# Mixer kernel on one core: all channel groups of five batches by block products, and a written order for the engines

## The chip, the core and the metric

The kernel runs on one core of a Trainium2 chip. A core has five engines that run at once, each through its own list of instructions in order: TensorE (PE, matrix products into PSUM; its weight loads are shown apart as PEld), VectorE (DVE), ScalarE (ACT), GpSimd (POOL) and SyncE (SP, which here only starts transfers). PSUM has eight banks of 512 fp32 columns. Engines wait for one another by semaphores. The metric is the device time of one execution in microseconds: the median of several runs.

## The reference

Inputs are q, k and v of shape 8 x 8 x 576 x 64 (batch, head, token, head column) and four weight matrices, all fp32. For each batch and head a linear attention is computed:

```python
phi(x) = where(x > 0, x, exp(x) - 1) + 1
kv  = phi(k)^T v                 # 64 x 64 per head
z   = sum of phi(k) over tokens
x   = (phi(q) kv) / (phi(q) z + 1e-6)
```

The heads of a batch side by side make x, 576 tokens by 512 channels. Then follows a mixer:

```python
h  = max(x^T w_tok1, 0) w_tok2   # 576 -> 256 -> 576, over tokens
u  = x + h^T
h2 = max(u w_ch1, 0) w_ch2       # 512 -> 1536 -> 512, over channels
out = u + h2
```

`max(u w_ch1, 0)` is called the first channel mixing here and the product with `w_ch2` the second.

## The kernel before, in words

Everything is computed in bf16 with fp32 sums. A batch's 576 tokens are four blocks of 128 (the main part) and 64 more; the 64 of two batches are handled together as one block of 128 (the "tails": `mm2_tails`, `mm3_tail`, `mm3_tails`, `tail_product`, `mm4` with t = 8).

The steps for batch n are these. SP loads q, k and v in halves of 576 KB (`load`), each into one fp32 buffer for all batches from 2 on. `phi_exp` (L148) takes the exponential on ScalarE, `phi_add` (L154) and `phi_end` (L161) finish phi on VectorE as min(exp(x), max(x + 1, 1)); `e` has four buffers, `y` two. `vcast` (L174) casts v. `kv` (L184) multiplies on TensorE, ScalarE copies the sums. From batch 2 on phi(q) is transposed by a DMA from SP's queue (`qtr_dma`, L219). `nd_all` (L252) makes numerators and denominators on TensorE and divides on VectorE. `mm1` (L306) and `mm2` (L317) mix over tokens; VectorE adds x to give u, and a transposing DMA (`utr_dma`, L519) makes uT.

The first channel mixing has twelve column blocks of 128, each four matmuls of 512 columns (`mm3`, L535), read by a ScalarE activation that clamps at zero (L550) into `cr`. Its output can also be computed by blocks: the inner 512 channels, the 1536 output channels and the tokens are each cut in two, and instead of eight block products seven are formed of sums and differences of blocks (a Winograd form of Strassen's method). The 1536 columns make three groups of 2 x 256 for this. In batches 2 to 6 the kernel does so for group 2 only (`mix_one`, L702): sums of weight blocks are made once (`group_sums`, L696, into `swc`), four sums of u blocks per batch (`u_sums`, L686, into `tuc`), then per group seven products of four matmuls of 256 columns. Products 1, 6 and 5 are copied to fp32 `part` buffers by ScalarE (L720), 4 is clamped by ScalarE (L718), and 2, 3 and 7 are read by VectorE, which adds the copied part and clamps (`add_relu`, L530). In batch 7 all three groups are done in this way (`mix_first`, L730).

The second channel mixing of batches 1 to 7 uses seven products too (`pair_product`, L839; `product`, L755): `row_sums` (L657) makes sums of `cr` blocks on VectorE into `sb`, which lies in the buffers of batch 1's v and q. For batches 1 to 6 ScalarE copies three partial products (`pair_copy`, L856), VectorE adds u (`pair_end`, L859), POOL adds the copies (L863), and POOL's queue writes the batch out in two transfers of 512 KB (`pair_put`). The output buffer `obuf` has eight slots, given out in turn. Batch 0 has a direct second mixing (`mm4`), and its first mixing too is direct.

The order of the work is the order in which the code issues it. Up to batch 6 `run` (L1060) walks a list of large TensorE pieces and issues, behind piece i, the smaller steps put at i (numbers such as `put(7, ...)`). The last batch follows a string of short names, `SEQUENCE` (L873). PSUM banks come from two rings, or from small tables. Batch 7's outputs leave in 24 transfers of 64 KB from SP's and ScalarE's queues (`product_read`, L798; `tail_read`, L834).

Of the kernel before, what the change touches and what calls it, by code (L numbers as in the profile page):

```python
# [15 lines left out]
EPS = 1e-6  # L16


@with_exitstack
def kernel(  # L20
# [43 lines left out]
    ring = {1: 0, 2: 0}  # L64

    def bank(at=None):
        if at is None:
            at, ring[1] = ring[1], (ring[1] + 1) % 4
        return psum[:, at]

    def banks(at=None):
        if at is None:
            at, ring[2] = 4 + ring[2], (ring[2] + 2) % 4
        return psum[:, at:at + 2]

    def two16():
        return banks().bitcast(BF16).rearrange("p a (t s) -> p a t s", s=128)
# [24 lines left out]
    uTj = [t.rearrange("p r j c -> p (r j c)").rearrange("p (j r c) -> p j r c", j=NDM, r=R) for t in uT]  # L102
    uTt = const("uTt", [128, 2, NDM, 128])
    cr = [const(f"cr{b}", [128, NCH, SM]) for b in range(2)]
    crt = const("crt", [128, NCH, 128])
    obuf = const("obuf", [128, 8, DM], FP32)
    swc = const("swc", [128, 4, 2, 256])
# [31 lines left out]

    live = {}  # L140
    o_at = [0]

    def o_slots(m):
        at = o_at[0] if o_at[0] + m <= 8 else 0
        o_at[0] = (at + m) % 8
        return obuf[:, at:at + m]

    def phi_exp(nm, n, j0, nj):  # L148
        f = raw[nm, rb(n)][:, j0:j0 + nj].rearrange("p j f -> p (j f)")
        e = work.tile([128, 2 * TD], BF16, name="e", tag="e", bufs=4)[:, :nj * TD]  # L150
        nc.scalar.activation(out=e, in_=f, func=AF.Exp)  # L151
        live["e", nm, n, j0] = e

    def phi_add(nm, n, j0, nj):  # L154
        f = raw[nm, rb(n)][:, j0:j0 + nj].rearrange("p j f -> p (j f)")
        y = work.tile([128, 2 * TD], BF16, name="y", tag="y")[:, :nj * TD]
        nc.vector.tensor_scalar(out=y, in0=f, scalar1=1.0, scalar2=1.0, op0=ALU.add, op1=ALU.max)  # L157
        for j in range(nj):
            live["y", j0 + j] = y[:, j * TD:]

    def phi_end(nm, n, j0, nj):  # L161
        c, i = divmod(j0, 2)
        dst = (kp if nm == "k" else qp)[:, c, :, i:i + nj]
        e, y = live["e", nm, n, j0], live["y", j0][:, :nj * TD]
# [4 lines left out]
    def phi(nm, n, c):  # L169
        phi_exp(nm, n, 2 * c, 2)  # L170
        phi_add(nm, n, 2 * c, 2)
        phi_end(nm, n, 2 * c, 2)
# [39 lines left out]
    def qtr(n, c, put=nc.scalar.copy):  # L212
        tp = two16()
        for h, ts in enumerate(TS):
            qtr_mm(c, ts, tp[:, h])
# [1095 lines left out]
```

## Time and profile before

| | us |
|---|---|
| median of 3 runs (lowest to highest) | 247.29 (247.22 to 247.83) |
| span of the profiled execution, first to last instruction | 246.4 |
| TensorE busy | 236.1 |
| VectorE busy | 198.8 |
| ScalarE busy | 139.3 |
| GpSimd busy | 76.9 |
| first mixing of batch 2 begins | 86.3 |
| first mixing of batch 7 begins | 214.3 |
| last VectorE addition begins | 242.7 |

No other time of the profiled execution is given than its span. The profile's page gives busy times, the span in 40 slices (tenths busy), the transfer queues, the chain of work that ended last, and the costliest groups of instructions by line. The views asked besides are a table of busy time by stage, the timeline of one engine, the waits, and the chain in order of time. Busy time of TensorE is not work at full rate, since matmuls overlap: the distance from one start to the next is its pace. The same holds for VectorE, where an instruction starts up to 0.1 us before the one in front has ended.

### The profile page before, as it was taken

What the parts mean: (1) busy time and instruction counts of PE and PEld (TensorE: products, weight loads), DVE (VectorE), ACT (ScalarE), POOL (GpSimd) and SP (SyncE); (2) the same over time, 40 slices, a digit from 0 to 9 for tenths busy, and PEclk for the clock granted to TensorE, in tenths of its full rate; (3) what the DMA queues carried; (4) which work ended last, traced back from release to release, by engine and by line L of the source; (5) the groups of instructions that cost most, each with busy time, mean ns of one, the idle gap of its engine ahead of it and who ended that gap; (6) DMA issues with size and microseconds to landing.
All of it is one profiled execution on the core that took longest, in us unless ns stands there. A gap on an engine that the chain in (4) does not pass through costs nothing.

```text
span 246.4 us, 6090 instructions
## 1 busy us (share of the span) xinstructions
PE 236.1 (96%) x2477; PEld 162.3 (66%) x2496; DVE 198.8 (81%) x349; ACT 139.3 (57%) x224; POOL 76.9 (31%) x88
## 2 busy tenths in 40 slices
PE   7789999999999899999999999999999999999993
PEld 3475455564868456865678556865676567888883
DVE  5955877889799998988894499979996779956973
ACT  4673881569774367736897167656852652175100
POOL 9670030296703600061004500071007700440360
PEclk9999999999999999999999999999999999999999
DMA  6999999999726796589979955459748702352055
GB/s 248 267 203 258 348 275 308 355 251 289 294 24 133 223 334 271 132 224 210 358 263 174 412 148 192 93 115 329 228 89 94 170 3 43 64 112 61 4 127 130
DMA packets 50444, 48.40 MB, mean 196 GB/s; under 512 B 30192, under 2 KB 36720, under 8 KB 50416
## 3 DMA queue, kind: packets, MB, share of 16 engines
q1 hardware_dynamic: 41984, 35.00, 48.2%
q0 software_dynamic: 7472, 12.22, 22.7%
q10 hardware_dynamic: 960, 0.79, 1.4%
q8 instruction: 19, 0.31, 0.5%
q14 instruction: 9, 0.07, 0.1%
HBM read 35.85 MB, written 9.44 MB: 184 GB/s over the span
## 4 chain that ended last, share of the span: by engine, by line
PE 84%; DVE 6%; DMA 5%; issue 3%; ACT 1%; SPq 0%; DVEq 0%
PE ps L543 22%; PE ps L852 18%; PE ps L712 6%; PE ps L312 6%; PE ps L583 5%; PE ps L740 4%; PE ps L768 4%; PE ps L325 4%; DMA q_raw<-in_q_dram 3%; PE ps L557 2%; PE ps L570 2%; DMA uT<-u 2%; PE ps L820 2%; PE ps L261 2%; PE ps L191 1%
## 5 line engine op out<-in xcount | busy, mean ns | idle before, releaser
L543 PE MATMUL ps<-uT,wc 128*128 128x512 bf16 x252 | 60.2, 379 | 0.8 <-DMA uT<-u 0.5
L550 ACT ACTIVATE cr<-ps 128x512 bf16<-128x512 f32 x59 | 34.7, 600 | 32.9 <-PE ps L543 32.7
L543 PEld LDWEIGHTS <-wc 128*128 128x128 bf16 x256 | 24.1, 98 | 25.1 <-DMA uT<-u 0.8
L863 POOL TENSOR_TENSOR obuf<-obuf,q_raw 128x512 f32<-128x512 f32 x6 | 8.1, 1344 | 93.3 <-DVE obuf L861 59.1
L852 PE MATMUL ps<-k_raw,v_raw 128*128 128x256 bf16 x216 | 24.9, 273 | 0.0
L852 PEld LDWEIGHTS <-v_raw 128*128 128x128 bf16 x216 | 21.0, 98 | 3.9 <-issue 0.4
L852 PEld LDWEIGHTS <-cr 128*128 128x128 bf16 x216 | 21.1, 98 | 3.7
L861 DVE TENSOR_TENSOR obuf<-ps,u 128x512 f32<-128x512 f32 x24 | 16.3, 685 | 8.1 <-PE ps L852 5.8
L151 ACT ACTIVATE e<-q_raw 128x1152 bf16<-128x1152 f32 x16 | 18.3, 1163 | 7.3 <-DVE x L244 5.5
L151 ACT ACTIVATE e<-k_raw 128x1152 bf16<-128x1152 f32 x16 | 18.2, 1165 | 2.7 <-DMA k_raw<-in_k_dram 2.7
L852 PE MATMUL ps<-wc,cr 128*128 128x256 bf16 x144 | 17.7, 273 | 0.0
L276 DVE TENSOR_TENSOR x<-ps,dens 128x768 bf16<-128x768 f32 x18 | 17.2, 953 | 0.4
L655 DVE TENSOR_TENSOR v_raw<-cr 128x768 bf16<-128x768 bf16 (+2 forms) x24 | 14.8, 617 | 2.1 <-ACT cr L718 2.1
L337 DVE TENSOR_TENSOR u<-ps,x 128x1024 bf16<-128x1024 f32 x12 | 14.6, 1217 | 0.4 <-PE ps L325 0.3
L176 ACT CAST vs<-v_raw 128x1152 bf16<-128x1152 f32 x12 | 13.5, 1161 | 0.0
L312 PE MATMUL ps<-x,w 128*128 128x512 bf16 x49 | 13.0, 379 | 0.3
L165 DVE TENSOR_TENSOR qp<-e,y 128x1152 bf16<-128x1152 bf16 x16 | 11.9, 753 | 1.6 <-ACT e L151 0.9
L165 DVE TENSOR_TENSOR kp<-e,y 128x1152 bf16<-128x1152 bf16 x16 | 12.7, 816 | 0.5 <-ACT e L151 0.4
L157 DVE TENSOR_SCALAR y<-k_raw 128x1152 bf16<-128x1152 f32 x16 | 11.7, 763 | 1.3 <-DMA k_raw<-in_k_dram 1.3
L157 DVE TENSOR_SCALAR y<-q_raw 128x1152 bf16<-128x1152 f32 x16 | 12.4, 793 | 0.4 <-DMA q_raw<-in_q_dram 0.4
L325 PE MATMUL ps<-ar,w2p 128*128 128x512 bf16 x44 | 11.8, 379 | 0.3
L583 PE MATMUL ps<-wc,cr 128*128 128x512 bf16 x47 | 11.9, 379 | 0.1
(182 smaller groups left out, 458.8 us busy)
## 6 DMA issues: line engine op xcount, KB each, us to landing
k_raw<-in_k_dram SPq DMA_DIRECT2D x16, 576.0 KB, 7.6
q_raw<-in_q_dram SPq DMA_DIRECT2D x16, 576.0 KB, 5.9
v_raw<-in_v_dram SPq DMA_DIRECT2D x14, 576.0 KB, 9.2
out_dram<-obuf POOLq DMA_DIRECT2D x12, 512.0 KB, 6.9
wc<-in_moe_w_ch_dram POOLq DMA_DIRECT2D x8, 384.0 KB, 9.8
out_dram<-obuf POOLq DMA_DIRECT2D x4, 256.0 KB, 6.0
out_dram<-obuf ACTq DMA_DIRECT2D x12, 64.0 KB, 2.2
out_dram<-obuf SPq DMA_DIRECT2D x12, 64.0 KB, 1.9
```

Of the source, the lines that this page charges most:

```text
L151: nc.scalar.activation(out=e, in_=f, func=AF.Exp)
L157: nc.vector.tensor_scalar(out=y, in0=f, scalar1=1.0, scalar2=1.0, op0=ALU.add, op1=ALU.max)
L165: live["phi"] = nc.vector.tensor_tensor(out=dst.transpose([0, 2, 1, 3]), in0=e.rearrange("p (i t d) -> p i t d", i=nj, t=T), in1=y.rearran ...
L276: nc.vector.tensor_tensor(out=xv[:, :, rc0:rc0 + 3], in0=v_[m][:, :, k0:k0 + 6, 0:D].rearrange("p i (q a) d -> p i q a d", a=2), in1=den.r ...
L312: nc.tensor.matmul(out=ps[:, mt], lhsT=w1t[:, b, ms] if r == R else w1[:, r, ms], rhs=x[b][:, r, :], start=(r == 0), stop=(r == R))
L325: nc.tensor.matmul(out=ps[:, i], lhsT=w2v(kt, r, b), rhs=ar[b][:, kt, :], start=(kt == 0), stop=(kt == NT - 1 and not add))
L543: nc.tensor.matmul(out=ps, lhsT=wc1[:, kj, 128 * mc:128 * mc + 128], rhs=uTj[b][:, kj] if n < 2 else uT[b][:, :, kj], start=(kj == 0), sto ...
L550: nc.scalar.activation(out=cr[b][:, mc, :], in_=ps, func=AF.Relu)
L583: nc.tensor.matmul(out=ps, lhsT=crt[:, kc, :] if t == 8 else cr[b][:, kc, 128 * r:128 * r + 128], rhs=wc2[:, kc, :], start=(kc == 0), stop ...
L655: return engine.tensor_tensor(out=s_[which - 1][:, ks], in0=x_, in1=y_, op=op)
L852: nc.tensor.matmul(out=live[tile_][:, j], lhsT=lhs[:, k_], rhs=rhs[:, k_], start=(first and j == 0 and k_ == 0), stop=(k_ == KH - 1), skip ...
L861: nc.vector.tensor_tensor(out=o, in0=live[tile_], in1=u[n % 2][:, d::2, HC[c]], op=ALU.add)
```

## The change

1. In batches 2 to 6 all three groups of the first channel mixing go by seven block products (`mix_mm`, `mix_read`), where before only group 2 did. `swc` holds weight sums of three groups (`GSW`). Groups 0 and 1 keep their copied parts in the first 2 KB per partition of each of the four row-sum buffers (`HOLD`), group 2 in `part` as before.
2. The issuing of every step is cut into small named tokens (`put`), and one string, `ORDER`, lists all of them after the setup; it replaces the lists and `SEQUENCE`. A token name is the batch, a letter for the step and an index: `4x26` is product 6 of group 2 of batch 4, `4y26` its read, `5gu1` the addition that makes half of batch 5's u, `5uT1` its transposing DMA, `4s2` a sum of u blocks, `4w10` a row sum, `4eW` an output addition, `6Lk0` a load. The order differs from before on every engine and on the queues of SP and POOL. Batch 1's loads are issued in the order k, v, q (before: k, q, v).
3. The PSUM bank of every result is named in a table (`BANK`), likewise output slots (`SLOT`), exp buffers (`EBUF`) and y buffers (`YBUF`). `obuf` has six slots (before eight), `e` three buffers (four), `y` one (two). The pair outputs of batches 1 to 6 all use slots 0 to 3.
4. The row sums 1 and 2 of batches 2 to 6 are cut into blocks of 2 and 4 (before 3 and 3).
5. Batch 7's outputs leave in 16 transfers: where `WHOLE` names a row of blocks, both halves of the columns go in one transfer of 128 KB, after the later half is done.

```diff
+NO = 6
+NE = 3
+NY = 1
+GSW = {2: 0, 1: 1, 0: 2}
+HOLD = {2: 'p0 p1 p2', 1: 's2 s3 s2', 0: 's0 s1 s0'}
+CUTS = {1: [0, 3, 6], 2: [0, 2, 6], 3: [0, 2, 6], 4: [0, 2, 6], 5: [0, 2, 6], 6: [0, 2, 6], 7: [0, 2, 4, 6]}
+GATE = {'1k0': ('wc1', 0), '2q0': ('wc2', 1), '4q0': ('u', 2, 1), '7q0': ('u', 5, 1)}
+ON_DVE = {'1v0', '2v1', '0r3', '0r6', '0r9', '1r5', '1r8'}
+WHOLE = {'00', '01', 't0', 't1'}
...
+1Lk0 1Lk1 1Lv0 A40 1Lv1 A41 1Lq0 A42 A43 1Lq1 0ma0 At2 0ma1 At3 0ma7
...
+5o0 5ne 6Lv1 4y11 4x25 3eW 4x21 6qx0 5n2 3hW 3p41 4y21 3p40 5n1 W1 4x01 4y25 5o1 4x26 6kb0 4y01 4x02 4y26 3eX
+4x16 6qx1 4x12 4y02 3o 4x27 6qa1 4x06 4y16 4x15 4y12 4y06 4x17 6qb1 4y15 4x05 6v0 6qa0 4x07 4x23 4y27 5f0 4y05
...
+    def mix_mm(n, g, i):
+        first = i in (1, 2, 5)
         b = n % 2
+        ps = mix_tile(n, g, i)
+        if n == B - 1:
+            s_, t, c0 = sw, tu, 256 * g
+        else:
+            s_, t, c0 = [swc[:, GSW[g], w] for w in range(4)], tuc, 0
+        w_ = lambda m, h: cblock(m, h)[:, :, 256 * g:]
         lhs, rhs = {1: (w_(0, 0), ublock(0, 0, b)), 2: (w_(0, 1), ublock(1, 0, b)),
+                    3: (s_[3][:, :, c0:], ublock(1, 1, b)), 4: (w_(1, 1), t[3]),
+                    5: (s_[0][:, :, c0:], t[0]), 6: (s_[1][:, :, c0:], t[1]),
+                    7: (s_[2][:, :, c0:], t[2])}[i]
...
+    def mix_read(n, g, i):
+        ps = mix_tile(n, g, i)
+        if n == B - 1:
+            c1, c6, c5 = hold[g]
         else:
+            c1, c6, c5 = [hold_at[w[0]][int(w[1])] for w in HOLD[g].split()]
+        dst = lambda m, e: cr[n % 2][:, KH * m + 2 * g:KH * m + 2 * g + 2, HALF[e]]
         if i == 4:
             nc.scalar.activation(out=dst(1, 0), in_=ps, func=AF.Relu)
         elif i in (1, 6, 5):
...
+    def product_put(n, i, j, e):
+        o = slots(f"{n}P{j}", 2)
+        d, c = {2: (0, 0), 7: (1, 1), 3: (0, 1), 4: (1, 0)}[i]
+        w = slice(0, 512) if f"{j}{d}" in WHOLE else HC[c]
+        [nc.sync, nc.scalar][e].dma_start(out=outv[n, :, 2 * (2 * j + d) + e, w],
+                                          in_=o[half[e], d, w])
...
+    for name in ORDER.split():
+        tok[name]()
```

## The prediction

> **What bounds the kernel now.** I read the page's busy table and its forty slices first.
>
> ```profile
> span 246.4 us, 6090 instructions
> ...
> PE 236.1 (96%) x2477; PEld 162.3 (66%) x2496; DVE 198.8 (81%) x349; ACT 139.3 (57%) x224; POOL 76.9 (31%) x88
> ...
> PE   7789999999999899999999999999999999999993
> ...
> DVE  5955877889799998988894499979996779956973
> ACT  4673881569774367736897167656852652175100
> ...
> PEclk9999999999999999999999999999999999999999
> ...
> PE 84%; DVE 6%; DMA 5%; issue 3%; ACT 1%; SPq 0%; DVEq 0%
> ```
>
> TensorE is the bound: 96% busy, 84% of the chain, full clock. But VectorE's row is almost as dense in the middle, so I asked for the busy time by stage, cut where a batch's first channel mixing begins (columns: stage, length, then busy time and count of PE, PEld, DVE, ACT, POOL).
>
> ```profile
> 53.30:86.30 33.00, 32.12 (x434) 21.07 (x436) 30.45 (x48) 22.38 (x34) 17.03 (x18) 1.00 0.69 206
> 86.30:109.17 22.87, 22.77 (x229) 15.90 (x232) 21.16 (x35) 15.35 (x23) 3.32 (x4) 1.00 0.75 233
> 109.17:139.15 29.98, 29.82 (x333) 20.87 (x334) 22.27 (x37) 20.14 (x30) 7.21 (x8) 1.00 0.95 275
> 139.15:164.41 25.26, 25.16 (x277) 17.15 (x278) 22.75 (x38) 16.47 (x25) 3.98 (x5) 1.00 0.59 171
> 164.41:189.60 25.19, 24.60 (x272) 16.83 (x272) 21.97 (x37) 14.47 (x23) 5.56 (x6) 1.00 0.75 182
> 189.60:214.33 24.73, 24.62 (x206) 16.66 (x209) 20.83 (x35) 9.71 (x17) 7.98 (x11) 1.00 0.36 74
> ```
>
> These are batches 2 to 6, behind the stretch that leads into them. TensorE idles 0.1 to 0.6 us a batch; VectorE has only 2 to 4 us free in 25 (7.7 in the stage with the leftover rows). So the gain must be read on TensorE, and its price on VectorE. The groups that carry both:
>
> ```profile
> L543 PE MATMUL ps<-uT,wc 128*128 128x512 bf16 x252 | 60.2, 379 | 0.8 <-DMA uT<-u 0.5 <-issue 0.2
> ...
> L712 PE MATMUL ps<-crt,swc 128*128 128x256 bf16 x60 | 8.2, 273 | 0.0
> ...
> L531 DVE CUSTOM_DVE_ANT_0 cr<-ps,part 128x512 bf16<-128x512 f32 x6 | 4.1, 688 | 2.5 <-PE ps L740 1.6 <-ACT part L720 0.8
> ...
> L550 ACT ACTIVATE cr<-ps 128x512 bf16<-128x512 f32 x59 | 34.7, 600 | 32.9 <-PE ps L543 32.7
> ```
>
> A matmul's 379 or 273 ns is latency. The pace comes from the chain: four of 512 columns take 0.86 us (0.215 each), eight of 256 take 0.87 (0.109). VectorE's clamps (688 ns) start 0.60 apart when back to back (95.14, 95.75, 96.34 in the timeline).
>
> **The change part by part.**
>
> *TensorE.* In batches 2 to 6 groups 0 and 1 change from direct products to seven block products, as group 2 has now. Per group 16 matmuls of 512 columns go (16 x 0.215 = 3.44 us), 28 of 256 come (28 x 0.109 = 3.05): 0.39 us saved. Ten groups: **-3.9 us**. Weight loads rise by 12 a group; each takes 98 ns beside a product's 109, so they stay hidden, with 11 ns to spare.
>
> *ScalarE.* Four clamps of 600 ns go per group; three copies of 579 to 588 and one clamp of 591 come: nil, and 57% busy covers it. But its queue is in order: an exponential (1.16 us) that waits for a load now holds copies that free a PSUM bank.
>
> *VectorE.* Per group three add-and-clamp reads of PSUM come: 3 x 0.605 = 1.82 us; ten groups 18.2 us. Weight combinations for two more groups are eight adds of 0.34 us (84.00 to 84.34): 2.7 us, or up to 4.3 if the first pair is slow as now (762 mean). They are placed in batches 0 and 1, where VectorE idles 7.4 of 30.8 us (22.5 to 53.3): taken as hidden; uncovered they cost their 2.7.
>
> With nothing moved, the batch 4 stage would have 25.16 - 0.78 = 24.4 us on TensorE and 22.75 + 3.63 = 26.4 on VectorE: VectorE would be the bound by 2 us a batch. So the redrawn order decides. I counted the instructions of each engine between the first block products of successive batches in the new order, at the start-to-start times above and those of the same timeline (phi steps 0.67, block normalisations 0.88, u additions 1.13, output additions 0.61, row sums 0.50 and 0.87). Checked on before from 141.53 to 166.78: VectorE is occupied 25.25 - 1.98 listed idle = 23.27 us where such a count gives 22.3, so I raise VectorE by 4.3%.
>
> TensorE against VectorE, in us: up to batch 2's mixing 63.6 and 61.2; batch 2 24.8 and 25.2; batch 3 26.2 and 26.8; batch 4 25.5 and 26.8; batch 5 23.6 and 23.8; batch 6 20.8 and 18.7; batch 7 until its last row sums 19.0 and 15.2. The order has spread VectorE's work forward (batch 4's phi and batch 3's normalisation stand before batch 2's first block product), but in four batches VectorE is still over by 0.4 + 0.6 + 1.3 + 0.2 = 2.5 us. Bounds: below, 0, if VectorE enters them ahead by the 2.4 us it has free before; above, 2.5 plus VectorE's own waits, which in before are 2.0 us a batch (four batches: 10.5). The row nearest to the new state is the batch 4 stage, where three of four idle pieces are VectorE waiting for TensorE or ScalarE; they shrink when VectorE is the late one. I take half the excess, **+1.2 us**.
>
> *Buffers.* Three exp buffers for four and one y buffer for two: each min must precede the next add, both on VectorE in that order anyway. Output slots shrink from 8 to 6 and the pair outputs of batches 1 to 6 all use slots 0 to 3. A batch's 512 KB writes land in 6.9 us; the next batch's first output addition is over 10 us later: nil under that cover, some 2 us without it. The held partial products of groups 0 and 1 lie in the row-sum buffers, so ScalarE's copy waits for the previous batch's last products, which the order puts first.
>
> *POOL and SP queues.* Nothing is added to POOL, but its 18 output additions (1.27 us) now run beside a fuller VectorE. The row is 78.91: two min steps took 2.49 us instead of 1.42 while a POOL addition took 1.71. One collision in 18 additions now; it sits inside the 4.3% and the upper bound. The Trainium skill (SBUF — State Buffer, "Who interferes with whom") says that VectorE instructions with two SBUF inputs, or in a two-port mode, and GpSimd lock each other out for a whole instruction. By that page alone, an estimate of half an addition (0.64 us) lost on each of batches 2 to 6's 15 would be 9.6 us, which would undo the change; the rows show such a loss once.
>
> *Loads at the start.* Batch 1's q moves behind v on SP's queue. Two 576 KB transfers at the slices' 300 GB/s are 3.9 us. The second quarter of the second mixing's weights waits for q's first half: now 30.4, then 34.3; it landed 6.5 us after (SP's next load is released at 36.96), with less beside it perhaps 4: 38.3 to 40.8. Its first product ran near 39.2 and stands near 39.0 in the new order. From 0 to 1.8; I take **+0.5**, nearer to the lower end since half the traffic beside it is gone. What queues behind is batch 2's loads and then ScalarE's exponentials.
>
> *Transposes.* Each batch's u goes through SP's transposing DMA, 3.0 to 5.2 us to landing. In the new order the first sum that needs it stands 4.3 to 5 us of VectorE work after the last u addition: nothing at 3.1, about 1 us a batch at 5.2. Taken as nil, in the upper bound.
>
> *The end.* 24 output transfers of 64 KB become 16, eight of them 128 KB. The last pair is twice as large: 128 KB more at the 200 GB/s of the last microseconds is +0.6; eight issues of about 0.55 on two queues go, at most -0.5 since the last one hardly queues now. Taken as 0.
>
> Sum: -3.9 + 1.2 + 0.5 = -2.2 on the profiled span of 246.4 gives 244.2. The median of the runs, 247.29, stands 0.9 above the span; the profiled execution has no other time, so I keep that: **245.1 us**.
>
> **The rivals.**
>
> *VectorE paces the middle and the kernel is slower.* The place is batches 2 to 5, in the wait of TensorE for PSUM banks that a VectorE clamp has to free. Price: the 2.5 us excess and 1 us of waits in each of five batches: -3.9 + 2.5 + 5 = +3.6, so 250.9. For it: VectorE at 95% and over, in order, with POOL and DMA delays it cannot catch up. Against it: the two engines are level to a few per cent, and most of its waits today are for TensorE. It decides once VectorE's waits in the middle exceed 3.9 - 2.5 = 1.4 us.
>
> *The full gain.* VectorE runs ahead and TensorE's 2.15 us of idle between 22.5 and 231.68 goes too: 247.3 - 3.9 - 2.15 = 241.2. For it: the order is written per instruction, with a bank named for every product. Against it: no stage leaves VectorE more than 2 us.
>
> *Gain and losses cancel* (the 2.5 us excess and 1.4 us of loads or transposes): 247.3.
>
> That the products are not reduced is excluded: their number is in the code.
>
> **How the numbers follow.** 0.3% is 0.74 us, about what a measurement of this kernel can tell from no change. Chances: the forecast case and the full gain 0.60 together (241.2 to 246.5, the forecast's own range 242.5 to 246.5), cancelling 0.12, VectorE-paced or late loads 0.28. Cutting 0.1 at each side gives 242.0 to 250.0.
>
> **What would show it.** Right: the block products of batches 2 to 6 are 420 matmuls instead of 140, DVE busy near 220 us (198.8 + 18.2 + 2.7), batches 2 to 6 about 2 us shorter together, PE over 96%. Wrong: TensorE waiting in those batches for VectorE (PSUM banks) with several tenths at a time; VectorE's min steps far above 750 ns; a stall near 39 to 47 us from the weights' or batch 2's q load; a last transfer landing over 3.7 us after the last addition.

## The result: slower by 0.75%, and the profile after

The changed kernel takes 248.99 us (median of four runs, 248.81 to 250.22) against 247.34 us: a ratio of 1.0075, 95% interval 1.005 to 1.0101. Faster by 2.2 us was forecast; the range held the time, the sign was wrong.

The page of the changed kernel, the same lines as were read before:

```profile
span 247.3 us, 6399 instructions
...
PE 235.2 (95%) x2616; PEld 174.3 (70%) x2616; DVE 214.4 (87%) x387; ACT 136.2 (55%) x224; POOL 81.2 (33%) x88
...
PE   7899998999899999899999999999999999999992
...
DVE  5956698899999999989999899989999869869862
...
PE 60%; DVE 6%; DMA 5%; issue 2%; ACT 0%; SPq 0%; DVEq 0%
```

VectorE has its forecast load (214.4 us of busy time, 220 expected), ScalarE and POOL are as they were. TensorE's share went down, not up. (The chain can be followed back only to 60.9 us here, so its shares don't compare with those of before.) The clock stayed at full speed as long as TensorE worked, so that is not it. The groups show that the products did what they should:

```profile
L679 DVE CUSTOM_DVE_ANT_0 cr<-ps,v_raw 128x512 bf16<-128x512 f32 x30 | 20.2, 685 | 4.0 <-PE ps L926 3.9
...
L926 PE MATMUL ps<-crt,swc 128*128 128x256 bf16 x180 | 22.7, 273 | 0.0
L684 PE MATMUL ps<-uT,wc 128*128 128x512 bf16 x96 | 22.2, 379 | 0.0
...
L926 PE MATMUL ps<-uT,wc 128*128 128x256 bf16 x144 | 19.8, 273 | 0.5 <-DVE x L411 0.3 <-DMA uT<-u 0.2
```

The direct products of 512 columns in this mixing fell from 252 recorded to 96, those of batches 0 and 1. Block products of 256 columns stand in their place, and the clamps' 685 ns is the 688 of before. By the paces (0.2157 and 0.109 us from one start to the next) that is 3.9 to 4.0 us less work. The stages (length, then busy time and count of PE, PEld, DVE, ACT, POOL) show where it stayed:

```profile
22.50:55.00 32.50, 31.12 (x261) 16.36 (x260) 26.40 (x55) 19.29 (x28) 11.86 (x11) 1.00 1.00 303
...
86.30:112.49 26.19, 25.42 (x312) 20.23 (x310) 24.61 (x41) 17.21 (x26) 4.08 (x4) 1.00 0.91 220
```

Between 22.5 and 55 us TensorE idles 1.4 us (0.2 before the change), in batch 2 0.8. Its last product ends at 242.56 us, before the change at 242.63: all that was saved is gone by then. (The execution profiled before was itself a long one, since every other execution took 1.7 to 1.9 us more than its span: by that the one with a span of 246.4 took about 248.2, not 247.3. In p_before below, profiled at 247.28 us, the last product ends at 241.7.) Behind 22.5 us, TensorE's waits in the timeline (start, length, instruction, and in brackets the idle time ahead and what ended it) are few and in separate places:

```profile
35.57 0.68 PE L318 MATMUL ps<-identity,qp 128*128 128x128 bf16 x9 [0.32 <-DVE qp L260]
37.82 0.41 PE L350 MATMUL ps<-kvbd,qT 128*128 128x130 bf16 x4 [0.71 <-ACT qT L324]
39.08 1.02 PE L745 MATMUL ps<-wc,cr 128*128 128x512 bf16 x4 [0.35 <-DMA wc<-in_moe_w_ch_dram]
...
67.73 1.47 PE L968 MATMUL ps<-wc,cr 128*128 128x256 bf16 x12 [0.79 <-DVE x L411]
...
104.07 1.14 PE L968 MATMUL ps<-k_raw,v_raw 128*128 128x256 bf16 x9 [0.77 <-DVE ut L481]
...
138.67 0.52 PE L385 MATMUL ps<-kvbd,qT 64*128 64x65 bf16 x22 [0.35 <-DMA qT<-qp]
...
165.58 1.05 PE L926 MATMUL ps<-uT,wc 128*128 128x256 bf16 x8 [0.18 <-DMA uT<-u]
166.91 1.03 PE L926 MATMUL ps<-uT,wc 128*128 128x256 bf16 x8 [0.28 <-DVE x L411]
```

A bracket counts from the modelled end of the product before. Counted by the paces, from one start to the next, the idle times are 0.50, 0.88 and 0.52 at the start, then 0.95, 0.93, 0.52, 0.34 and 0.46 us: 5.1 in all. The kernel before has three such places, 1.8 us counted in the same way:

```profile
61.50 0.81 PE L543 MATMUL ps<-uT,wc 128*128 128x512 bf16 x3 [0.16 <-issue]
...
85.50 0.67 PE L261 MATMUL ps<-kvbd,qT 64*128 64x65 bf16 x33 [0.62 <-DVE obuf L610]
...
189.61 0.60 PE L543 MATMUL ps<-uT,wc 128*128 128x512 bf16 x2 [0.50 <-DMA uT<-u]
```

Behind TensorE the end has grown too: from the end of the last addition to the end of the span it is 4.3 us (243.01 to 247.3), 3.3 before.

Two theories follow. **W**: TensorE still paces the kernel, and the gain is given back at these places, each with its own cause. **V**: VectorE paces the middle, as in the first rival on record, and the waits only show where TensorE has run ahead.

### The profile page after: what moved, and what is told of

The parts are those of the page before. It is cut to its first block, busy times and chain, and to the rows that moved or that the text cites. A ratio compares the mean times of both kernels' runs of the same rounds, so it can differ in the third digit from the quotient of the medians.

```text
span 247.3 us, 6399 instructions
## 1 busy us (share of the span) xinstructions
PE 235.2 (95%) x2616; PEld 174.3 (70%) x2616; DVE 214.4 (87%) x387; ACT 136.2 (55%) x224; POOL 81.2 (33%) x88
## 4 chain that ended last, share of the span: by engine, by line
PE 60%; DVE 6%; DMA 5%; issue 2%; ACT 0%; SPq 0%; DVEq 0%
PE ps L926 21%; PE ps L968 21%; PE ps L446 5%; PE ps L457 3%; DMA uT<-u 3%; PE ps L731 2%; DMA qT<-qp 2%; DVE u L468 2%; PE ps L1022 2%; PE ps L709 2%; PE ps L385 1%; PE ps L745 1%; PE ps L300 1%; DVE y L254 1%; DVE x L411 1%
## 5 line engine op out<-in xcount | busy, mean ns | idle before, releaser
L968 PE MATMUL ps<-k_raw,v_raw 128*128 128x256 bf16 x252 | 31.5, 273 | 0.8 <-DVE ut L481 0.8
L941 ACT COPY v_raw<-ps 128x512 f32<-128x512 f32 x30 | 17.0, 592 | 26.0 <-PE ps L926 22.2
L926 PEld LDWEIGHTS <-swc 128*128 128x128 bf16 x240 | 23.4, 98 | 3.8
L926 PEld LDWEIGHTS <-wc 128*128 128x128 bf16 x216 | 21.0, 98 | 4.2 <-DMA uT<-u 0.5
L679 DVE CUSTOM_DVE_ANT_0 cr<-ps,v_raw 128x512 bf16<-128x512 f32 x30 | 20.2, 685 | 4.0 <-PE ps L926 3.9
L926 PE MATMUL ps<-crt,swc 128*128 128x256 bf16 x180 | 22.7, 273 | 0.0
L684 PE MATMUL ps<-uT,wc 128*128 128x512 bf16 x96 | 22.2, 379 | 0.0
L926 PE MATMUL ps<-uT,wc 128*128 128x256 bf16 x144 | 19.8, 273 | 0.5 <-DVE x L411 0.3
L1069 POOL TENSOR_TENSOR obuf<-obuf,w 128x512 f32<-128x512 f32 x6 | 8.4, 1405 | 30.5 <-ACT w L1056 20.7
L834 DVE TENSOR_TENSOR v_raw<-cr 128x512 bf16<-128x512 bf16 (+3 forms) x24 | 14.9, 640 | 2.0 <-ACT cr L939 1.8
L684 PEld LDWEIGHTS <-wc 128*128 128x128 bf16 x96 | 9.0, 98 | 10.3 <-issue 1.0
L446 PE MATMUL ps<-x,w 128*128 128x512 bf16 x56 | 14.4, 379 | 0.0
```

What stands on the lines that cost most here:

```text
L446: nc.tensor.matmul(out=banks(f"{n}f")[:, mt], lhsT=w1t[:, b, ms] if r == R else w1[:, r, ms], rhs=x[b][:, r, :], start=(r == 0), stop=(r = ...
L679: nc.vector._custom_dve(TENSOR_ADD_SAT, out=o, in0=ps, in1=c, s0=3.4028234663852886e38, s1=0.0)
L684: nc.tensor.matmul(out=bank(f"{n}m{mc}"), lhsT=wc1[:, kj, 128 * mc:128 * mc + 128], rhs=uTj[b][:, kj] if n < 2 - U1 else uT[b][:, :, kj], ...
L834: return engine.tensor_tensor(out=s_[which - 1][:, ks], in0=x_, in1=y_, op=op)
L926: nc.tensor.matmul(out=ps[:, j], lhsT=lhs[:, k_, 128 * j:128 * (j + 1)], rhs=rhs[:, :, k_], start=(first and j == 0 and k_ == 0), stop=(k_ ...
L941: nc.scalar.copy(out={1: c1, 6: c6, 5: c5}[i], in_=ps)
```

## The experiments

Each figure is a median, and the ratio is that to the kernel before in the same session, with its 95% interval. Differences between runs are those of the medians; medians of different sessions can stand a few tenths apart.

### One group back to direct products (e_direct0)

```diff
-{n}x01 ... {n}x07, {n}y01 ... {n}y07      (n = 2 to 6: seven products, seven reads)
+{n}m0 {n}m1 {n}m6 {n}m7, {n}r0 {n}r1 {n}r6 {n}r7   (four direct products, read by ScalarE)
```

> The changed kernel with group 0 of batches 2 to 6's first channel mixing by direct products again: 80 matmuls of 512 columns for 140 of 256 columns (TensorE +1.95 us by the paces 0.2157 and 0.109) and 15 add-and-clamp reads of VectorE less (-9.1 us). Theory W (TensorE paces, VectorE's share costs at most some tenths): slower by 1 to 2 us, 250.0 to 251.0. Theory V (VectorE paces batches 2 to 5): as fast or faster than with all groups in seven products, 247.0 to 249.2, with TensorE waiting less for VectorE in batches 2 to 5.

251.60 us, 1.0171 [1.015, 1.0193]. TensorE's last product ends at 244.82 instead of 242.56 us: +2.26 for five groups, 0.45 a group where 0.39 was worked out. That figure has waits in it. TensorE's idle time comes to about the same as in the changed kernel (5.2 us by the paces), but in other places: the waits at 103 and 138 us are gone, and a long one stands where the changed kernel has its two at 165 and 166 us, behind the same transposed u, which landed 7.7 us after its issue.

```profile
167.39 0.82 PE L925 MATMUL ps<-uT,wc 128*128 128x256 bf16 x6 [1.56 <-DVE x L410]
```

Taking 9 us off VectorE (7.8 by the busy times) brought nothing back. The products are worth their price on TensorE; V has a bad start.

### The exponential ahead of a copy (e_exp)

The wait at 103 to 104 us is put down to VectorE's `ut`. ScalarE's timeline says otherwise:

```profile
99.77 0.76 ACT L306 CAST kvbd<-ps 64x260 bf16<-64x260 f32 x2
102.24 1.17 ACT L250 ACTIVATE e<-k_raw 128x1152 bf16<-128x1152 f32 x1 [1.71 <-DMA k_raw<-in_k_dram]
103.43 0.59 ACT L1056 COPY q_raw<-ps 128x512 f32<-128x512 f32 x1
```

The copy at 103.43 takes batch 2's first partial product out of PSUM; the next product adds into the same bank and can't start before it ends, at 104.02. TensorE starts at 104.07. The copy stood behind an exponential that waited 1.71 us for batch 5's k. One name moves:

```diff
-... 2w10 5kx0 2w12 3g0 2w20 2c0 2w22 ...
+... 2w10 2w12 3g0 2w20 2c0 5kx0 2w22 ...
```

> The changed kernel with one instruction moved on ScalarE's queue: the exponential of batch 5's first k half goes behind batch 2's first partial-product copy. Theory W (the 3.9 us are gained on TensorE and given back in a handful of separate waits, one of which is this: the exponential waits 1.71 us for its load and holds the copy, for which TensorE waits 0.9 us at 103.1): TensorE's gap at 103 to 104 us goes from 0.93 to under 0.2, and the time falls by 0.5 to 0.9, to 248.1 to 248.5. Theory V (VectorE paces batches 2 to 5, and the gap merely shows where TensorE has run ahead): the gap comes back within a few microseconds, on a VectorE result, and the time stays within 0.2 of 249.0.

248.26 us, 1.003 [1.002, 1.0039]: 0.7 us back from one instruction (1.1 by the ratios). In its timeline the copy runs ahead of the exponential, and the product starts without a wait:

```profile
101.24 0.59 ACT L1056 COPY q_raw<-ps 128x512 f32<-128x512 f32 x1 [0.67 <-ACT kvbd L306]
102.74 1.16 ACT L250 ACTIVATE e<-k_raw 128x1152 bf16<-128x1152 f32 x1 [0.91 <-DMA k_raw<-in_k_dram]
...
103.17 1.47 PE L968 MATMUL ps<-k_raw,v_raw 128*128 128x256 bf16 x12
```

TensorE's end moves from 242.56 to 241.65, the whole 0.9. The exponential still waits, and costs nothing there. All runs of the changed kernel below hold this edit, but for e_end24 and e_start.

### GpSimd beside VectorE (e_sums)

In the changed kernel, VectorE and POOL ahead of the wait at 66.8 us:

```profile
62.40 1.71 DVE L260 TENSOR_TENSOR qp<-e,y 128x1152 bf16<-128x1152 bf16 x1
64.15 1.60 DVE L254 TENSOR_SCALAR y<-q_raw 128x1152 bf16<-128x1152 f32 x1
65.67 0.17 DVE L398 TENSOR_SCALAR dens<-ps 128x28 f32<-128x28 f32 x1
...
60.94 2.60 POOL L762 DMA_DIRECT2D out_dram<-obuf  x4
63.55 3.22 POOL L814 TENSOR_TENSOR q_raw<-wc,q_raw 128x512 f32<-128x512 bf16 x2
```

Two VectorE steps of 0.75 us take 1.71 and 1.60 around POOL's weight sums (L814), and batch 2's normalisation stands behind them. By the rows the first step should have ended at 63.15, ahead of the sums' start at 63.55, but times on POOL are rough; the edit decides it. It makes the sums wait for the second of these steps:

```diff
-        first = {(0, 0): ("phi", "q", 2, 1), (2, 0): ("phi", "k", 2, 1)}.get((i, k0))
+        first = {(0, 0): ("phi", "q", 2, 1), (2, 0): ("phi", "k", 2, 1),
+                 (2, 4): ("add", "q", 3, 1)}.get((i, k0))
```

> The changed kernel with the moved exponential, and GpSimd's last three weight sums held until VectorE's second y step of batch 3's q has been done, so that they run beside batch 2's normalisation, whose VectorE steps read PSUM. Theory L (GpSimd and VectorE hold each other up only where VectorE works from SBUF; the sums lengthen two VectorE steps from 0.75 to 1.71 and 1.60 us, the normalisation starts 1.8 us late and TensorE waits 0.95 us at 66.8): the two steps fall to 0.75, TensorE's gap there to under 0.2, the time by 0.6 to 1.0 against the 248.26 of the exponential alone, to 247.3 to 247.7. Rival (VectorE would be late there in any case, or the sums lengthen the normalisation as much): no gap closed, time within 0.3 of 248.26.

247.10 us, 0.9977 [0.9965, 0.9988]: 1.2 us less than e_exp, and faster than the kernel before.

```profile
62.44 0.74 DVE L260 TENSOR_TENSOR qp<-e,y 128x1152 bf16<-128x1152 bf16 x1
63.22 0.93 DVE L254 TENSOR_SCALAR y<-q_raw 128x1152 bf16<-128x1152 f32 x1
64.19 0.19 DVE L398 TENSOR_SCALAR dens<-ps 128x28 f32<-128x28 f32 x1
...
64.24 3.53 POOL L814 TENSOR_TENSOR q_raw<-wc,q_raw 128x512 f32<-128x512 bf16 x3 [0.67 <-DVE y L254]
...
66.83 1.36 PE L968 MATMUL ps<-wc,cr 128*128 128x256 bf16 x11
```

POOL issues its transfers beside the first step in both kernels (at 60.9, for 2.6 us), so it was the sums that lengthened it. TensorE's wait at 66.8 is gone. The normalisation starts at 64.19 instead of 65.67, and its VectorE steps, which read PSUM, keep their times beside the same sums (0.90 us for the multiplications, 0.94 elsewhere).

### Transposes beside loads (e_transp)

SyncE's queue in the changed kernel, ahead of the waits at 138 and 165 us:

```profile
130.12 3.25 SPq L487 DMA_TRANSPOSE uT<-u  x2
133.42 1.40 SPq L333 DMA_TRANSPOSE qT<-qp  x1
...
157.63 0.42 SPq L226 DMA_DIRECT2D v_raw<-in_v_dram  x1
158.10 1.67 SPq L487 DMA_TRANSPOSE uT<-u  x1
```

The transpose at 133.42 landed 5.2 us later, the one at 158.10 7.4 us later, with four loads of batch 7 issued between 156.89 and 160.97 around it. (The wait at 166.91 is put down to VectorE's `x`; VectorE had itself waited 1.1 us for this transpose.) The edit also puts batch 7's first q exponential later, beside its second.

```diff
-GATE = {..., '7q0': ('u', 5, 1)}
+GATE = {..., '7q0': ('u', 5, 0), '6v0': ('q', 5, 1)}
-... 5qT0 ... 4uT0 ... 4uT1 ... 5qT1 ...   7Lq1 5gt 7Lv1 6K 4w22 5uT0 ... 7Lq0 ... 7Lv0 ... 5ut
+... 5qT0 5qT1 ... 4uT0 ... 4uT1 ...       5gt 6K 4w22 5uT0 ... 5ut 7Lq0 7Lv0 7Lq1 7Lv1
```

> The changed kernel with the moved exponential, and with the transposes freed from loads: the second transpose of batch 5's q goes ahead of those of batch 4's u on SyncE's queue and batch 6's first v load waits for it; batch 7's q and v loads go behind the transposes of batch 5's u. Theory T (transposes that queue behind others or run beside loads take 5.2 and 7.4 us instead of 3.1 to 3.7, and TensorE waits 0.52 + 0.34 + 0.46 us for them at 138, 165 and 166 us): these gaps go, the time falls by 0.8 to 1.3 against 248.26, to 247.0 to 247.5. Rival (the loads that are put off are late next, an exponential waits for them and holds ScalarE's queue): the gaps move to later batches, time 248.0 to 249.0.

247.07 us, 0.9969 [0.9957, 0.9981]: 1.2 us less than e_exp. The two transposes land in 3.8 us at most and 4.5 us, and no wait of TensorE is left between 137 and 170 us:

```profile
137.28 0.79 PE L385 MATMUL ps<-kvbd,qT 64*128 64x65 bf16 x40
...
163.89 1.91 PE L926 MATMUL ps<-uT,wc 128*128 128x256 bf16 x16
```

The loads that were put off hold nothing up. The edit does two things, the order of the transposes and the later loads; no run separates them.

### Without any transpose (p_base, p_before)

To see what transposes cost in all, they are replaced by copies of the same bytes, in the changed kernel with the moved exponential (p_base) and in the kernel before (p_before). This leaves the transposition out, so phi(q) and u reach the products untransposed and the output is not the reference's: in the runs named p_ the times alone count, and that a gain found there holds beside real transposes is not shown.

```diff
-        live["u", n, i] = nc.sync.dma_start_transpose(...)
+        live["u", n, i] = nc.sync.dma_start(...)        # so too for qT and the tails' uTt
```

> The changed kernel with the moved exponential, and with its 27 transposing transfers replaced by plain copies of the same bytes between the same tiles, which leaves the transposition out (phi of q and u reach the products untransposed). It is the base of the three runs beside it. Theory T (TensorE waits for transposes at 138, 165 and 166 us, 1.3 us in all, and nowhere else): the time is that of the kernel with its transposes freed from loads, 247.07, within 0.4. Rival (the transposes hold up more than is seen there, through SyncE's queue and the transfers beside them): under 246.5.

> The kernel before, with its 27 transposing transfers replaced by plain copies of the same bytes, which leaves the transposition out. Theory T (the transposes cost the kernel before almost nothing, since its order left them 2 us more): 247.0 to 247.6, no more than 0.5 under the kernel before. Rival (they cost both kernels the same, and 1.3 us in the changed one is no part of the error): 246.0 to 246.5.

p_base 246.90 us, 0.9974 [0.9959, 0.9988]; p_before 247.32 us, 0.9994 [0.9982, 1.0007]. Waiting for transposes cost the changed kernel 1.4 us (248.26 to 246.90) and the one before nothing that the medians show (its one wait for a transpose is the 0.50 us at 189.61). p_base is the base of the p_ runs below.

### VectorE's load (p_light)

```diff
-2qa0 2qa1 2ka0 2ka1 ... 7qa0 7qa1         (24 y steps)
```

> The base with plain copies, and without the y steps (max(x + 1, 1)) of batches 2 to 7: the min steps read what batch 1 left, so phi is not the reference's. 24 VectorE instructions of 0.75 us (16 us at their pace of 0.67) go, nothing else changes. Theory W (VectorE's load as such costs little; TensorE waits for it at one place, 66.8 us, because of GpSimd's sums): that gap closes, the time falls by 0.6 to 1.3 under the base. Theory V (VectorE paces batches 2 to 5): TensorE's small waits go in all stages, the time falls by 2 us or more.

247.29 us, 0.9998 [0.9976, 1.002]: 16 us less on VectorE, and not faster than its base. At batch 3's normalisation (its products at 81.26 instead of 82.37 us) it was 1.1 us ahead, and at batch 6's (159.65 instead of 160.76) no more than that. The whole gain is the wait at 66.8 us, which is closed here too, as W has it. Then:

```profile
164.74 1.51 DVE L881 TENSOR_TENSOR crt<-uT,crt 128x512 bf16<-128x512 bf16 x1
166.17 1.82 DVE L259 TENSOR_TENSOR kp<-e,y 128x1152 bf16<-128x1152 bf16 x1
...
164.70 1.26 POOL L1067 TENSOR_TENSOR obuf<-obuf,w 128x512 f32<-128x512 f32 x1 [2.47 <-DVE obuf L1060]
165.92 1.45 POOL L1067 TENSOR_TENSOR obuf<-obuf,part 128x512 f32<-128x512 f32 x1
```

In the base these two POOL additions start at 168.70 and 169.92, and the two VectorE steps take 0.41 and 0.75 us. With POOL on top of them they take 1.51 and 1.82, and TensorE waits for them and what stands behind them (0.30 us at 166.30, 0.58 at 169.45). So V is out for this order: from batch 3 to batch 6 VectorE's load as such took nothing. The delays of VectorE that were found to cost time, here and at 66.8 us, stand where an instruction of it met one of POOL.

### The end (e_end24, e_end12, p_end20)

First guess: go back to 24 transfers. Those of block row 0 (`j` in `product_put`) and of the tails go behind their last additions; the eight of block row 1, which were 64 KB all along, keep the places that the changed order gave them.

```diff
-WHOLE = {'00', '01', 't0', 't1'}
+WHOLE = set()       # 7D20. 7D30. 7D70. 7D40. behind 7R20 .., 7td2. .. behind 7tr2 ..; 7D21. 7D31. 7D71. 7D41. as changed
```

> The changed kernel with its last batch's outputs in 24 transfers of 64 KB again, each issued right after its last addition; the rest as changed. Theory E (the end is 0.9 us longer since the last pair of transfers is 128 KB instead of 64 KB): the span behind the last addition falls from 4.3 to about 3.3 us and the time from 249.0 to 248.1 (ratio to the kernel before 1.004). Rival (the 128 KB is not what takes the time, the transfers queue in any case, and eight more issues cost as much): the last landing moves by less than 0.3 us, 248.7 to 249.3.

250.07 us, 1.0106 [1.0088, 1.0123]: slower still. The guess fell. Its last addition ends at 243.32, but ScalarE's queue goes on issuing, one each 0.65 us:

```profile
242.91 0.61 ACTq L989 DMA_DIRECT2D out_dram<-obuf  x1
243.61 0.55 ACTq L1036 DMA_DIRECT2D out_dram<-obuf  x1
244.25 0.55 ACTq L989 DMA_DIRECT2D out_dram<-obuf  x1
244.90 0.56 ACTq L1036 DMA_DIRECT2D out_dram<-obuf  x1
```

The first of these four is 7D211, whose addition was long done, and another such late one, 7D711, is among ScalarE's last eight issues: 1.3 us at this pace. So the expectation's "each issued right after its last addition" does not hold for block row 1, and whether 24 well-placed issues would keep up is not shown. From the last issue on it is 3.4 us here (244.90 to 248.3), 4.0 in the changed kernel (243.28 to 247.3) and 3.1 before: the smaller last transfers did gain 0.6, and the late queue lost 1.3. Second try, 12 transfers from all 128 partitions at once:

```diff
-outv[n, :, 2 * (2 * j + d) + e, w]                          # in_=o[half[e], d, w]
+outv[n, :, r:r + 2, w].rearrange("p e w -> e p w")          # in_=o[:, d, w]
```

> The changed kernel with the moved exponential, and with the last batch's outputs in 12 transfers of 128 KB, one behind each last addition, from 128 partitions at a time and on SyncE's and ScalarE's queues in turn. Theory Q (24 transfers failed since ScalarE's queue was still issuing 1.9 us after the last addition, at 0.65 us each; 16 end late since the last two carry 256 KB): issues end with the last addition, the last 128 KB land like the kernel before's, 3.3 us from the end of the last addition to the end of the span instead of 4.3, and the time falls by 0.7 to 1.0 against 248.26, to 247.3 to 247.6. Rival (a transfer of 128 KB on one queue takes as long as two of them at once): 248.0 to 248.6.

261.94 us, 1.0572 [1.0558, 1.0586]. This tells nothing of the queues: written so, all transfers in flight move at 47 to 50 GB/s together, and one of 128 KB lands 14.4 us after its issue. The Trainium skill (DMA: Bandwidth & Descriptors, "Why a DMA increments its semaphore by 16 and not by 1") says that a transfer is spread over the largest number of engines up to 16 that divides the slowest dimension of both sides. On the side of the output that dimension is 2 here, 128 on the other. The trace agrees: in those slices the 16 engines are busy for one tenth on average. By the page's 436 GB/s for sixteen engines an estimate for two is 54.5. Third try, 20 transfers, each pair issued at once, and 64 KB in each transfer of the last three pairs:

```diff
+WHOLE = {'00', 't0'}     # 7D21. 7D31. 7D71. 7D41. 7D70. 7D40. 7td7. 7td4. behind 7R.., 7tr.
```

> The base with plain copies, with the last batch's outputs in 20 transfers, every pair issued right behind the addition that completes it, whole rows only where both halves are done early, and 64 KB for each of the last four pairs. Theory Q (the last 512 KB go out in 2.1 us at the 314 to 335 GB/s of the slices, so the size of what is left at the last two additions sets the end, as long as ScalarE's queue has issued all before): from the last addition's end to the span's end 3.3 to 3.7 us instead of 4.3, time 0.5 to 0.9 under the base. Rival (four more issues at 0.65 us put the queues behind again, as with 24): 4.3 us or more, no gain.

245.91 us, 0.9934 [0.9909, 0.9959], 1.0 us under p_base. From the last addition to the end of the span it is 3.4 us (242.49 to 245.9), 4.4 in p_base. The last issue starts 0.2 us behind the last addition, and 3.2 us are left from there, 4.1 in p_base. So what gains here is less data in the last transfers; e_end24 shows the other half, that the queues must have issued everything ahead of them.

### The start (e_start, e_start2, p_kqv, p_kqv2, p_nocomb, p_all_nocomb)

TensorE's three waits at 35 to 39 us come from batch 1's q, now loaded behind v, and from the weights of the second mixing that wait for q. e_start ties these weights to v instead and draws two steps ahead to fill the gaps; e_start2 also puts two of VectorE's combinations later; p_kqv loads q first again, with batch 1's steps reordered to fit; p_kqv2 also alternates two pairs of banks and puts two more combinations later.

```diff
-            live["in", "q", 1, 0] if i == 1 else None)
+            live["in", "v", 1, 0] if i == 1 else None)      # e_start, e_start2
-1Lk0 1Lk1 1Lv0 1Lv1 1Lq0 1Lq1
+1Lk0 1Lk1 1Lq0 1Lq1 1Lv0 1Lv1                               # p_kqv, p_kqv2
-1n00:4 1n01:4 1n10:4 1n11:6 1n20:6 1n21:4
+1n00:6 1n01:6 1n10:4 1n11:4 1n20:4 1n21:6                   # p_kqv2
```

> The changed kernel with the second quarter of the second mixing's weights gated on batch 1's v instead of its q, and with two steps of batch 0's second mixing drawn ahead of batch 1's transposes and normalisation products. Theory W (late loads at the start leave TensorE idle 0.50 + 0.88 + 0.52 us between 35.1 and 39.1): these gaps shrink to under 0.5 in all, TensorE reaches the 55 us mark 1.2 to 1.9 us earlier, and the time falls by 0.9 to 1.9 to 247.1 to 248.1 if nothing behind takes it back. Theory V: TensorE is earlier at 55 us but not at batch 2's first mixing product (86.3 us), since VectorE's work up to there (57.3 us busy of 63.8, with its own waits for loads) does not move; time within 0.3 of 249.0.

> The changed kernel with the moved exponential and the earlier gate and moved mixing steps of the run before it, and with two of VectorE's weight combinations (the third of group 0 and the first of the second mixing) put behind batch 1's normalisation. Theory L (the earlier gate alone failed since GpSimd's weight sums then met VectorE's combination at 37.3 us, which took 1.38 instead of 0.42 us, and those 42.5 us: 1.93 instead of 0.95, both ahead of batch 1's normalisation): TensorE's gaps between 35 and 46 us fall from 1.9 to under 0.6 us in all, batch 2's normalisation products start at 62.1 instead of 63.4, and the time falls by 0.8 to 1.4 against 248.26, to 246.9 to 247.5. Rival (VectorE is the limit from 46 us on in any case): less than 0.3 gained.

> The base with plain copies, with batch 1's q loaded ahead of its v again, as before the change: phi of q, its transposes on TensorE and the gate of the second mixing's weights come 3.5 us earlier, batch 1's v casts and K-V products later; the three VectorE weight combinations there stand behind batch 1's normalisation. Theory S (the chain from batch 1's q to its normalisation is what TensorE waits for at 35 to 39 us, and only an earlier q shortens it): TensorE's gaps between 31 and 46 us fall from 2.0 to under 0.7 us in all, batch 2's normalisation products start at 62.0 to 62.5 instead of 63.46, time 0.8 to 1.4 under the base. Rival (v, now last, is late in the same way: its casts and the K-V products stand ahead of the same normalisation): within 0.3 of the base or slower.

> The base with plain copies (246.9), with batch 1's q loaded ahead of its v as in the run with that order before, and besides with batch 1's normalisation products in two pairs of PSUM banks in turn instead of one (the kernel before had two), two of VectorE's combinations more behind that normalisation, and a mixing step ahead of the second q transposes. Theory S (q's lateness and the one pair of banks make the chain): TensorE's gaps between 31 and 46 us fall from 2.3 to under 0.8 us in all, batch 2's normalisation products start at 62.0 to 62.5, time 245.5 to 246.2. Rival (the start is limited elsewhere, by when the weights land or by VectorE): 246.6 or more.

e_start 250.07 us, 1.0101 [1.0085, 1.0117]; e_start2 248.23, 1.0021 [1.0011, 1.0031], level with e_exp; p_kqv 247.47, 0.9995 [0.9981, 1.0008], and p_kqv2 247.73, 1.0003 [0.9992, 1.0014], both above p_base. None gained. In e_start the three waits have shrunk to one of 0.23 us, and others have come, the longest here (and 0.42 us at 45.52):

```profile
37.33 1.38 DVE L895 TENSOR_TENSOR swc<-wc 128x512 bf16<-128x512 bf16 x1
...
36.97 2.74 POOL L814 TENSOR_TENSOR q_raw<-wc 128x512 f32<-128x512 bf16 x2 [3.71 <-DVE swc L895]
...
39.80 0.40 PE L350 MATMUL ps<-kvbd,qT 128*128 128x130 bf16 x4 [1.18 <-DVE x L362]
```

The weights land earlier, so POOL's sums start earlier and meet a VectorE combination (1.38 us instead of 0.42) ahead of the normalisation. In e_start2 they hardly meet, and TensorE waits 0.64 us for the weights and 0.79 us for the normalisation itself. p_kqv2 reaches the first token mixing at 45.55 instead of 46.28 us and loses it again; p_all (below), which holds the same start, shows the place:

```profile
52.07 0.27 PE L517 MATMUL ps<-x,identity 128*128 128x256 bf16 x1 [1.14 <-DVE obuf L757]
```

Last, the eight weight combinations that the change adds to VectorE are left out, in both orders of the loads (on top of the two runs of the next section). Groups 0 and 1 then use the sums of group 2, so here too the times alone count:

```diff
-GSW = {2: 0, 1: 1, 0: 2}
+GSW = {2: 0, 1: 0, 0: 0}          # and no G01 ... G04, G11 ... G14
```

> The kernel with plain copies, sums held back and 20 transfers (245.31), without the eight VectorE weight combinations of groups 0 and 1 in batches 0 and 1: all groups use those of group 2, so the first channel mixing of groups 0 and 1 is not the reference's. Theory C (the combinations, 2.7 us of VectorE, are what holds the start): TensorE's gaps at 35 to 39 us close, batch 2's normalisation products start at 62.0 to 62.4 instead of 63.4, 244.0 to 244.5. Theory D (the late q and weights hold it, VectorE has room there): within 0.3 of 245.31.

> The kernel with plain copies, sums held back, 20 transfers and q loaded ahead of v (245.72), without the eight combinations. Theory C and D both (late loads in the one order, combinations in the other): only this one gets back to 62.0 to 62.4 at batch 2's normalisation products, 243.9 to 244.5. C alone: as the other run. If neither moves: something else holds the start, and it stays open.

245.12 us, 0.9902 [0.9875, 0.9928], against 245.31 with them: nothing in the changed order. 244.80 us, 0.9882 [0.9856, 0.9908], against 245.72: 0.9 with q first. Batch 2's normalisation products start at 63.30 and 63.39 in these two, at 63.36 and 64.02 with the combinations. So with q last it is not the combinations. With q first they cost, but even without them q first is no faster than q last beyond the intervals (244.80 and 245.12). What order would start these products at 62.1, as in p_before, was not found: the start stays open.

### The gains together (p_sumend, p_all)

p_sumend is p_base with the sums held back and 20 transfers; p_all has q first besides.

> The base with plain copies (246.9), with GpSimd's last three weight sums held back (-1.2 alone) and the 20 transfers at the end (-1.0 alone). Theory W (separate waits, each given back in full): the gains add, 244.5 to 245.0. Theory V (VectorE becomes the bound): 245.4 or more. A third way, seen when the y steps were left out: VectorE, earlier by 1 us, meets GpSimd elsewhere, two instructions of it take 1 us more each near 165 us, and 245.3 to 246.

> The base with plain copies with all three: q ahead of v with two pairs of banks, GpSimd's sums held back, 20 transfers. Theory W with S: 243.2 to 244.2, 3 to 4 us under the kernel before with plain copies, which is the whole of what the block products take off TensorE. Without S: as the run without the start's edit, 244.5 to 245. If VectorE or GpSimd take it: over 245.

245.31 us, 0.9898 [0.9881, 0.9915], and 245.72, 0.992 [0.9903, 0.9937]. The two gains (1.2 and 1.0 alone) give 1.6 together, with intervals of 0.4 us to each side, where W had 244.5 to 245.0. In the two profiled executions (247.13 and 244.98 us) they add in full: TensorE ends 1.2 us earlier, the end is 1.0 shorter, and TensorE has no wait near 165 us, so the meeting that the expectation's third way feared is not there. Against p_before p_sumend is 2.0 us faster. Of the 3.9 us of the block products some 1.9 are still missing; the three waits at the start, 1.9 us by the paces, are the only ones left behind 22.5 us, but p_before has 1.2 us of its own, so the sum does not close to the tenth. With real transposes, the sums and the transposes each cured alone already beat both kernels (0.9977, 0.9969); the four edits together with real transposes were not run.

## Why the prediction was wrong, step by step

| term | predicted | measured |
|---|---|---|
| TensorE, ten groups | -3.9 | -4.5 by 0.45 a group, waits included (e_direct0) |
| VectorE's excess in four batches | +1.2 (0 to 10.5) | 0 as a load (p_light) |
| POOL beside VectorE | inside the 4.3% | +1.2 (e_sums) |
| ScalarE's copies behind an exponential | nil | +0.7 (e_exp) |
| transposes | nil (to 1 a batch) | +1.2 to 1.4 (e_transp, p_base) |
| loads at the start | +0.5 (0 to 1.8) | 1.9 idle, not won back, cause open |
| the end | 0 (-0.5 to +0.6) | +1.0 (p_end20) |

With -3.9 the measured terms give about +2.1; the medians differ by +1.65. The terms were measured one at a time and need not add, so the 0.4 between stays open.

- **TensorE** was right, and so were the number of products and VectorE's load.
- **The step that failed is the price of the redrawn order.** The prediction looked for it in VectorE's sum of times. What turned the sign are four costs that it names and puts at nothing or into a percentage (ScalarE's queue, transposes, the end, POOL beside VectorE) and a fifth that it sized too low (the start): 0.7, 1.2, 1.0, 1.2 and 1.9 us measured, against 0.5 forecast for the start and nothing for the others.
- **VectorE's sum** was wrong too, but the other way. Counted per batch it came out 2.5 us over TensorE, and half of that was taken as the loss. A load 16 us smaller made nothing faster, so neither the 1.2 nor the rival's price of 7.5 us existed. Without it the forecast would have been 1.2 us further off; that the measured time lies in the stated range is in part luck. The first rival, the only slower one, named VectorE's clamps and their banks, and none of the changed kernel's eight waits was for those.
- **POOL and VectorE** were named, with the right row (two min steps in 2.49 us) and the rule beside it, and then folded into a percentage. The Trainium skill (SBUF — State Buffer, "Who interferes with whom") says that the one to issue first keeps the shared ports for its whole instruction, and that VectorE contends with two SBUF inputs or in a two-port mode. The trace agrees in which steps are slowed: the min step with two SBUF inputs lost 0.97 us and the y step with one 0.85, those that read PSUM nothing; that the y step runs in a two-port mode no run here shows. The 9.6 us estimated from the page was far too much; one meeting in a critical place was enough to cost 1.2.
- **ScalarE's queue**: the sentence that an exponential waiting for a load now holds copies that free a bank was right in mechanism; it was priced at nil, and one place cost 0.7 to 0.9.
- **Transposes**: the bound of about 1 us a batch held (0.5 us at 138, 0.8 at 165 and 166); "nil" was the wrong choice. The working looked at u alone, and one of the two late transposes is of q. There loads and other transposes stood around them.
- **The start**: right place, mis-sized. The estimate followed only the weights' landing (0 to 1.8); batch 1's own q chain, behind the same loads, was not followed, and it holds two of the three waits. That the later q is the cause is argued, not shown: loading it first again won nothing back (p_kqv, p_kqv2).
- **The end**: +0.6 for the larger last pair was cancelled against -0.5 for fewer issues. The last issue waits for the last addition in both kernels (243.34 and 243.28 us), so fewer issues could not pay.

The range held the time, since it reached to cases of late loads; the chance of 0.28 for slower was too small for four terms that were given no price and a fifth set low. The base was off as well: the 0.9 us between span and median belongs to two different executions (last section), so the term of 244.2 started from a long one.

## What to carry to other kernels

When an order is redrawn, don't compare engines by sums per stage: for each instruction moved, look at what stands behind it on its queue (a copy behind an exponential, a normalisation behind a min step) and at what runs on the neighbouring engine in that same microsecond. A cure that makes something earlier can cost as much as it gains, since it moves a whole queue beside another engine's critical steps (e_start, p_light); so measure cures one at a time and read where the wait went. Of several costs that are named and given no price, expect some to be real: here four of about 1 us each and a fifth set too low ate a saving of 3.9.

## What the runs showed of the hardware

- The releaser named for a wait can be a bystander: `ut` on VectorE ended at 104.04 us, the copy that TensorE waited for at 104.02. Moving the copy settled it.
- At the end, outputs of 64 KB with 1 KB of a row for each partition go out at about 200 GB/s (198 to 207 in each microsecond from 240 to 245 in e_end24), those of 128 KB with 2 KB rows at 307 (244 to 245 us in the changed kernel). That the row's size is the cause is not shown: two queues that issue 64 KB each every 0.65 us come to 202 GB/s as well.
- The quarter of weights at 39 us lands at different times: the profiled execution of p_end20 waited 1.53 us for it, and with 247.67 us was the slowest of seven whose median is 245.91.

```profile
40.79 1.02 PE L744 MATMUL ps<-wc,cr 128*128 128x512 bf16 x4 [1.53 <-DMA wc<-in_moe_w_ch_dram]
```

- The time stands 1.7 to 1.9 us above the span in every execution listed since; the 0.9 of the prediction compared the median with the span of another execution, one whose last product came 0.9 us later than p_before's.
